# Half of wo's first block on partitions 0 to 63, brought by two transfers of 32 partitions whose source counts in eights

## The chip, the core and the metric

The kernel runs on one core of one Trainium2 chip. The metric is the device time of one execution in microseconds (us). "Engine 0 to 15" means the 16 DMA engines of the core. TensorE is called PE, VectorE DVE, ScalarE ACT, GpSimd POOL and SyncE SP, as in the profile.

## The reference, cut to what matters

One decode step of attention over a long cache, mixed with a gated MLP. The caches are 2 x 268 MB and are read once; all else is small.

```python
def _A_ref(x, k_cache, v_cache, wq, wo):        # B=4, D=1024, H=32, Sk=8192, Dh=128
    q = ...(x @ wq)...
    scores = jnp.einsum("bhqd,bhkd->bhqk", q, k_cache) * (Dh ** -0.5)
    p = _softmax(scores, axis=-1)
    o = jnp.einsum("bhqk,bhkd->bhqd", p, v_cache)
    return o.transpose(...).reshape(B, Sq, H * Dh) @ wo      # wo: 4096 x 1024
...
g = _sigmoid((x * gate_w).sum(-1, keepdims=True))
return g * a + (1 - g) * b
```

## The kernel before

K and V stream through a ring of five slots in SBUF on the SP queue. `wo` comes last, in eight blocks of 512 rows (1 MB each). A block lies on 128 partitions, 4 rows (8 KB) on each; the matching rows of the attention's output are brought to the same partitions by small matmuls with slices of the identity (`o_rows`). Blocks 0 and 1 are queued ahead of the last piece of V, the others behind it, the last two in ever smaller cuts.

```python
    def o_rows(g0, g1):
        n = g1 - g0
        lp = small([P, FR, n, Bn])
        for k in range(WB):                     # WB = 4 heads in a block
            for r in range(FR):                 # FR = 4 rows on a partition
                nc.tensor.matmul(lp[32 * k:32 * k + 32, r], lhsT=identb[:, r:P:FR],
                                 rhs=OT[:, WB * g0 + k:WB * g1:WB, :], start=True, stop=True, skip_group_check=True)
        nc.vector.tensor_copy(out=LT[:, :, g0:g1, :], in_=lp[:])

    def wo_block(g, r0=0, r1=FR):
        home, at = divmod(g, 4)
        if home not in wo_home:
            wo_home[home] = ring[:, slots(1)].rearrange("p (g r n) -> p g r n", g=4, r=FR)
        w = wo_home[home][:, at]
        nc.sync.dma_start(out=w[:, r0:r1].rearrange("p r n -> p (r n)"),
                          in_=wov[:, g, r0:r1].rearrange("p r n -> p (r n)"))
        def use():
            for r in range(r0, r1):
                for n in range(NH):
                    mm_acc(acc[:, n * NB:(n + 1) * NB], LT[:, r, g, :], w[:, r, n * NB:(n + 1) * NB])
        return use
    # ... cut ...
        if (kind, d) == ("v", ND - 1):
            for g in range(2):
                wo_block(g)()
        if kind == "v":
            v_pair(d)
    # ... cut ...
    last = [wo_block(g) for g in range(2, NWB - 2)]
    cuts = [(NWB - 2, 0, 2), (NWB - 2, 2, 4), (NWB - 1, 0, 2), (NWB - 1, 2, 3), (NWB - 1, 3, 4)]
```

Another part matters for one experiment: `keep_weights` drops a weight load of PE that repeats the one before it.

Of the kernel before, what the change touches and what calls it, by code (L numbers as in the profile page):

```python
# [8 lines left out]
BF = mybir.dt.bfloat16  # L9
# [103 lines left out]
def kernel(  # L113
# [15 lines left out]
    nc = tc.nc  # L129
    P = 128  # L130
    Bn, Sq, D = A_x.shape
# [13 lines left out]
    FR = 4  # L145
    FG = F // (P * FR)
    NB = 512
    NH = D // NB
# [8 lines left out]
    const = ctx.enter_context(tc.tile_pool(name="const", bufs=1))  # L157
# [10 lines left out]
    ring = const.tile([P, NS, RING], BF, name="ring")  # L168
# [6 lines left out]
    def turned(rows, n, dtype=BF):  # L175
        t = TB[tb_turn[0] % 3]
        tb_turn[0] += 1
        return t[0:rows, 0:n] if dtype == BF else t[0:rows, 0:2 * n].bitcast(dtype)

    def slots(n):  # L180
        at = turn[0]
        turn[0] = (at + n) % NS
        return at
# [15 lines left out]
    def small(shape, dtype=F32):  # L199
        return mps.tile(shape, dtype, name="small", tag="small")  # L200
# [16 lines left out]
    acc = acc4[0:Bn].rearrange("p z n -> p (z n)")  # L217
# [3 lines left out]
    n = 1  # L221
# [6 lines left out]
    ident = const.tile([P, P], F32)  # L228
# [2 lines left out]
        nc.gpsimd.tensor_copy(out=ident[n:n + 32, n:n + 32], in_=id32[n:n + 32])  # L231
    identb = const.tile([P, P], BF)
    nc.vector.tensor_copy(out=identb[:], in_=ident[:])
    xw_ps = small([P, DT, NX], BF)
    for t in range(DT):
        nc.tensor.transpose(out=xw_ps[:, t, :], in_=x6[:, t:D:DT], identity=identb[0:NX, 0:NX])  # L236
# [4 lines left out]
    for half in range(2):  # L241
        for e in range(2):
            nc.gpsimd.tensor_copy(out=R[:, 2 * half + e].rearrange("p (n j) -> p n j", n=4),
                                  in_=ident[:, 64 * half + e:64 * half + 64:2].unsqueeze(1).to_broadcast([P, 4, 32]))
# [20 lines left out]
    qa = const.tile([P, 4, H, Bn], BF)  # L265
    OT = const.tile([P, H, Bn], BF)
    LT = const.tile([P, FR, H // FR, Bn], BF)
    hT = const.tile([P, FG, FR, Bn], BF)
    sgb = const.tile([P, 2, Bn], F32)
    c12 = const.tile([P, 2, Bn], F32)  # L270

    def mm_acc(out_ap, lhsT, rhs, start=False):
        nc.tensor.matmul(out_ap, lhsT=lhsT, rhs=rhs, start=start, stop=True, skip_group_check=True)  # L273
# [16 lines left out]
    def add_x():  # L290
        xf = turned(Bn, D, F32)
        nc.vector.tensor_copy(out=xf, in_=x6[0:Bn])
        for n in range(NH):
            mm_acc(acc[:, n * NB:(n + 1) * NB], dg[:], xf[:, n * NB:(n + 1) * NB])
# [67 lines left out]
# [4 lines that stand above are left out]
        for k in range(WB):  # L366
            for r in range(FR):
                nc.tensor.matmul(lp[32 * k:32 * k + 32, r], lhsT=identb[:, r:P:FR],  # L368
                                 rhs=OT[:, WB * g0 + k:WB * g1:WB, :], start=True, stop=True, skip_group_check=True)
        nc.vector.tensor_copy(out=LT[:, :, g0:g1, :], in_=lp[:])  # L370

    wo_home = {}

    def wo_block(g, r0=0, r1=FR):

# [12 lines that stand above are left out]
# [35 lines left out]
    def k_pair(d):  # L423
        g, t = divmod(d, GD)
        Z = Zt[d % 2]
        if d == 0:
            spread(0)
        if t == 0:
            S_ps[g] = scp.tile([P, 2, 512], F32, name="S_ps")
        sps = S_ps[g]  # L430
        ks = load_pair(kv_view(A_k_cache, d), RING)
        for n in range(RD):
            kn, c = ks[n // JT], n % JT
            flat_t = turned(P, CJ * P)
            T = flat_t.rearrange("p (j h i e) -> p j h i e", j=CJ, h=2, e=2)
            nc.vector.transpose(out=flat_t.bitcast(U32),  # L436
                                in_=kn[:, c * CJ * Dh:(c + 1) * CJ * Dh].bitcast(U32))
            s = QP - 1 - (RD * t + n)
            for he in range(4):
                half, e = divmod(he, 2)  # L440
                for z in range(2):
                    nc.tensor.matmul(sps[:, z, :], lhsT=Z[:, he, s:s + P], rhs=T[:, 16 * z:16 * z + 16, half, :, e],  # L442
                                     start=(t == 0 and n == 0 and he == 0),
                                     stop=(t == GD - 1 and n == RD - 1 and he == 3))
            if n == JT // 2 and d + 1 < ND:
                spread(d + 1)
            if n == JT:
                flush()
            if n == JT + 2:
                flush_late()  # L450
        if t == GD - 1:
            softmax(g)
# [101 lines left out]
    for kind, d in order:  # L554
        if kind == "k":
            k_pair(d)
            if d in side:
                side[d]()
        if (kind, d) == ("v", ND - 1):
            for g in range(2):  # L560
                wo_block(g)()
        if kind == "v":
            v_pair(d)
        if (kind, d) == ("k", ND // 2):
            add_x()
        if (kind, d) == ("v", ND - 2):
            o_rows(0, GE)
# [5 lines left out]
    flush_late()  # L573
    last.pop(0)()
    o_rows(GE, NWB)
    for use in last:
        use()
# [35 lines left out]
```

## Time and profile before

| | before |
|---|---|
| time, median (range) of 6 runs | 1344.05 us (1343.86 to 1344.24) |
| span of the profiled execution | 1342.2 us |
| PE busy | 77% of the span |
| instruction fetches of 16 KB | 27 |

The page of the kernel before, its slices (one figure for each 1/40 of the span; for DMA the busy share in tenths) and its table of DMA queues (packets, MB, share of 16 engines' time):

```profile
DMA  9999999999999999999999999999999999999997
GB/s 414 436 432 431 439 434 427 445 430 422 445 424 430 442 432 426 438 434 428 438 436 426 432 430 434 436 433 438 428 423 436 430 431 442 436 419 444 419 425 325
...
q1 hardware_dynamic: 14276, 575.69, 99.5%
q8 instruction: 27, 0.44, 0.1%
```

The DMA engines are busy for 90% or more of every slice before the last, so bytes, and how evenly they lie on the engines, set the time. The q8 line: 27 packets, 0.1% of the time.

The end of the chain of waits before (start us, length us, what):

```profile
1321.33 16.11 DMA ring<-in_A_wo_dram
1337.43 0.04 issue
1337.47 1.90 PE acc L273 x8
1339.37 0.02 issue
1339.40 0.57 ACT TB L581
```

The span ends on landings of wo, eight matmuls, a copy, and the output. The landing that is named is that of the third transfer of wo from the end (1337.43 us); the last two land at 1338.1 and 1338.7 us, while the eight matmuls run. All three show the same gaps between the engines. The timeline around block 0 (start us, length us, engine, line, what; in brackets the idle time before it and what ended it):

```profile
1306.32 0.22 DVE L370 CAST LT<-small 128x64 bf16<-128x64 f32 x1 [40.50 <-PE small L368]
1306.60 2.75 PE L273 MATMUL acc<-ring,LT 128*4 128x512 bf16 x12 [0.32 <-DVE LT L370]
...
1308.98 0.39 PE L513 MATMUL o_ps<-ring,PB 128*32 128x512 bf16 x1
...
1313.84 1.24 PE L513 MATMUL o_ps<-ring,PB 128*32 128x512 bf16 x5 [1.23 <-DMA ring<-in_A_v_cache_dram]
```

PE begins on the last V at 1308.98 us and has to wait for data 1.23 us at 1313.84 us.

Two things come from the trace's records and not from a view. A transfer adds 1 to its semaphore for each engine that finishes its share, so the 16 times of these completions show how far apart the engines are. And each packet has a start and a length; on one engine the packets follow each other without a gap. Before, the 16 completions of the last transfer of wo (us):

```
1332.3 1332.3 1332.4 1332.7 1332.9 1332.9 1333.2 | 1335.3 | 1336.9 1337.0 1337.0 1337.0 1337.2 | 1338.5 1338.7 1338.7
```

Seven engines are early, one is 3 us behind the first, and eight are 4.7 to 6.4 us behind. At 38 us the spread was 0.6 us. The lag grows in steps, one for each 16 KB fetch. Such a step, near 302 us (start, end, length in us, bytes, queue):

```
299.691 302.117 2.426 65536 q1      the packet before
302.114 303.173 1.059 16384 q8      the fetch
303.158 306.084 2.926 65536 q1      1.04 us later than without it, and 0.5 us longer
```

So one fetch costs its engine about 1.55 us. Eight engines take the fetches in turn: in the transfers that begin to land at 401, 808 and 1215 us, after 8, 16 and 24 fetches, eight engines are 1.6 to 2.0, 3.2 to 3.5 and 4.7 to 5.0 us behind the first. And 27 = 3 x 8 + 3: at the end five of the eight have three, three have four. PE and its weight loads have 4552 + 2364 = 6916 instructions by the page, or 256 for each of the 27 fetches: these are PE's instructions. The Trainium skill, "Runtime: NRT & Kernel Launch", section "Instruction fetch mechanics", says that instructions come in blocks of 16 KiB, 256 instructions each, and that crossing into the next block is "mostly hidden". The size agrees with this trace.

### The profile page before, as it was taken

The numbers are of one execution on the slowest core, as the hardware profiler recorded it, in microseconds if no ns is written. First come the engines' busy times: TensorE is split into PE (matmuls) and PEld (weight loads), VectorE is DVE, ScalarE is ACT, GpSimd is POOL, SyncE is SP. The second block draws the span as 40 slices with busy tenths as digits, with TensorE's granted clock in tenths as the row PEclk, the third lists the DMA queues.
The fourth block names the chain that finished last, engine by engine and source line by source line (L and its number), as shares of the span: only waits on it lengthen the run. The fifth ranks groups of instructions, "written<-read, shape, count | busy, mean of one in ns | idle before, by whom it ended". The sixth has DMA issues, their size and how long they took to land.

```text
span 1342.2 us, 7696 instructions
## 1 busy us (share of the span) xinstructions
PE 1032.8 (77%) x4552; PEld 227.9 (17%) x2364; DVE 614.4 (46%) x369; ACT 50.6 (4%) x46; POOL 62.8 (5%) x161
## 2 busy tenths in 40 slices
PE   2565878787788687778977779597778679877898
PEld 0111111111111121111211112111111112111221
DVE  2555655545336554335455556046555254556000
ACT  0000100001000010001000010000100010000100
POOL 2000100001000010001000010000100010000100
PEclk9787988888998888889988889888889899888899
DMA  9999999999999999999999999999999999999997
GB/s 414 436 432 431 439 434 427 445 430 422 445 424 430 442 432 426 438 434 428 438 436 426 432 430 434 436 433 438 428 423 436 430 431 442 436 419 444 419 425 325
DMA packets 14316, 576.18 MB, mean 429 GB/s; under 512 B 1598, under 2 KB 1606, under 8 KB 2252
## 3 DMA queue, kind: packets, MB, share of 16 engines
q1 hardware_dynamic: 14276, 575.69, 99.5%
q8 instruction: 27, 0.44, 0.1%
q14 instruction: 5, 0.04, 0.0%
q10 hardware_dynamic: 8, 0.00, 0.0%
HBM read 575.68 MB, written 0.01 MB: 429 GB/s over the span
## 4 chain that ended last, share of the span: by engine, by line
DMA 66%; DVE 21%; PE 11%; another core or an unknown queue 1%; ACT 0%; issue 0%; SPq 0%; DVEq 0%
DMA ring<-in_A_k_cache_dram 58%; DVE TB L436 21%; PE o_ps L513 9%; DMA ring<-in_A_v_cache_dram 5%; DMA x<-in_gate_w_dram 2%; DMA ring<-in_A_wo_dram 1%; PE S_ps L442 1%; ACT PB L484 0%; PE S_ps L307 0%; PE acc L307 0%; PE acc L273 0%; PE small L533 0%; ACT OS L525 0%; PE small L472 0%
## 5 line engine op out<-in xcount | busy, mean ns | idle before, releaser
L436 DVE STREAM_TRANSPOSE TB<-ring 128x2048 uint32<-128x2048 uint32 x256 | 566.9, 2277 | 492.4 <-DMA ring<-in_A_k_cache_dram 491.5
L442 PE MATMUL S_ps<-TB,Z 128*128 128x512 bf16 x2048 | 518.8, 408 | 219.4 <-DVE TB L436 218.9
L513 PE MATMUL o_ps<-ring,PB 128*32 128x512 bf16 x2048 | 461.4, 388 | 52.6 <-DMA ring<-in_A_v_cache_dram 48.1
L442 PEld LDWEIGHTS <-Z 128*128 128x128 bf16 x1024 | 105.4, 103 | 628.0 <-issue 626.4
L513 PEld LDWEIGHTS <-PB 128*32 128x32 bf16 x1024 | 100.7, 98 | 405.1 <-issue 393.7
L421 POOL COPY Z<-qa 32x4 bf16<-32x4 bf16 x128 | 25.6, 200 | 761.6 <-PE S_ps L442 736.0
L486 POOL COPY PB<-PT 32x1024 bf16<-32x1024 bf16 x16 | 30.3, 1892 | 430.3 <-PE o_ps L513 426.2
L467 ACT ACTIVATE PTs<-S_ps,mx 128x1024 bf16<-128x1024 f32 x8 | 8.9, 1114 | 1020.9 <-DVE mx L463 1020.9
L526 DVE SCALAR_TENSOR_TENSOR OS<-o_ps,mE,OS 128x512 f32<-128x512 f32 x8 | 6.0, 751 | 72.2 <-ACT OS L525 72.2
L484 ACT COPY PB<-PT 32x1024 bf16<-32x1024 bf16 x16 | 30.5, 1908 | 1.5 <-DVE PT L469 1.3
L474 DVE RECIPROCAL rinv<-small 128x16 f32<-128x16 f32 x8 | 2.1, 258 | 42.0 <-PE small L472 42.0
L370 DVE CAST LT<-small 128x64 bf16<-128x64 f32 x2 | 0.4, 224 | 42.3 <-PE small L368 42.3
L236 PE MATMUL small<-identb,x 6*128 6x6 bf16 x8 | 0.6, 195 | 22.3 <-DMA x<-in_gate_w_dram 22.3
L457 DVE TENSOR_REDUCE mx<-S_ps 128x1 f32<-128x1024 f32 x8 | 9.8, 1225 | 15.9 <-PE S_ps L442 15.9
L273 PE MATMUL acc<-ring,LT 128*4 128x512 bf16 x64 | 14.8, 379 | 1.7 <-DMA ring<-in_A_wo_dram 1.0
L469 DVE STREAM_TRANSPOSE PT<-PTs 128x1024 bf16<-128x1024 bf16 x8 | 10.0, 1245 | 10.2 <-ACT PTs L467 10.2
L273 PE MATMUL acc<-ring,hT 128*4 128x512 bf16 x56 | 12.2, 379 | 0.0
L525 ACT ACTIVATE OS<-o_ps,mE 128x512 f32<-128x512 f32 x8 | 5.5, 687 | 162.8 <-PE o_ps L513 162.8
L307 PE MATMUL o_ps<-ring,xw 128*4 128x512 bf16 x56 | 5.7, 536 | 5.3 <-DMA ring<-in_B_w_gate_dram 5.3
L533 PEld LDWEIGHTS small<-selg,OS 128*128 128x128 f32 x64 | 9.0, 208 | 4.1 <-issue 3.9
L533 PE MATMUL small<-selg,OS 128*128 128x16 f32 x64 | 8.7, 269 | 0.0
L238 DVE COPY xw<-small 128x48 bf16<-128x48 bf16 x1 | 0.2, 181 | 15.9 <-PE small L236 15.9
(64 smaller groups left out, 67.2 us busy)
## 6 DMA issues: line engine op xcount, KB each, us to landing
ring<-in_A_k_cache_dram SPq DMA_DIRECT2D x14, 4096.0 KB, 34.1
ring<-in_A_v_cache_dram SPq DMA_DIRECT2D x14, 4096.0 KB, 31.4
ring<-in_B_w_gate_dram SPq DMA_DIRECT2D x1, 7168.0 KB, 37.1
ring<-in_B_w_up_dram SPq DMA_DIRECT2D x1, 7168.0 KB, 39.2
ring<-in_B_w_down_dram SPq DMA_DIRECT2D x2, 3584.0 KB, 27.4
ring<-in_A_wo_dram SPq DMA_DIRECT2D x6, 1024.0 KB, 24.7
ring<-in_A_v_cache_dram SPq DMA_DIRECT2D x2, 2048.0 KB, 28.7
ring<-in_A_v_cache_dram SPq DMA_DIRECT2D x4, 1024.0 KB, 24.7
```

Source lines behind the costliest of these rows:

```text
L273: nc.tensor.matmul(out_ap, lhsT=lhsT, rhs=rhs, start=start, stop=True, skip_group_check=True)
L421: nc.gpsimd.tensor_copy(out=Z[at, :, QP - 1 + QP * q], in_=qa[at, :, h0 + q, b])
L436: nc.vector.transpose(out=flat_t.bitcast(U32), in_=kn[:, c * CJ * Dh:(c + 1) * CJ * Dh].bitcast(U32))
L442: nc.tensor.matmul(sps[:, z, :], lhsT=Z[:, he, s:s + P], rhs=T[:, 16 * z:16 * z + 16, half, :, e], start=(t == 0 and n == 0 and he == 0), ...
L457: nc.vector.tensor_reduce(out=mx[:, 0:1], in_=sps[:].rearrange("p z n -> p (z n)"), axis=AX.X, op=ALU.max)
L467: nc.scalar.activation(out=PTs[:], in_=sps[:].rearrange("p z n -> p (z n)"), func=ACT.Exp, bias=negm[:, 0:1], scale=scale, accum_out=rs[:, ...
L469: nc.vector.transpose(out=PT[:].rearrange("p j i -> p (j i)"), in_=PTs[:])
L484: nc.scalar.copy(out=Bv[at, :, :, q, :], in_=Pv[at])
L486: nc.gpsimd.tensor_copy(out=Bv[at, :, :, q, :], in_=Pv[at])
L513: nc.tensor.matmul(o_ps[row:row + NM, e, :], lhsT=PB[:, RD * t + c, z, w].rearrange("p e s j -> p (e s j)"), rhs=vn[:, j0 * Dh:(j0 + 4) * ...
L526: nc.vector.scalar_tensor_tensor(out=o_sb[:], in0=o_ps[:, 1, :], scalar=mE[:, 1:2], in1=o_sb[:], op0=ALU.mult, op1=ALU.add)
L533: nc.tensor.matmul(oT[:, :], lhsT=o_sb[:, q * Dh:(q + 1) * Dh], rhs=selg[:, q].rearrange("p t s -> p (t s)"), start=(q == 0), stop=(q == 3))
```

## The change

The intent, as far as the code shows it: move bytes from engines 8 to 15 to engines 0 to 7. Rows 0 to 255 come by two transfers onto partitions 0 to 63, whose source's outermost dimension has 8 steps; rows 256 to 511 come onto 128 partitions, 2 rows on each. `ident4` orders the rows of the attention's output to match. The diff, cut:

```diff
+    ident4 = const.tile([P, FR, 8, 4], BF)
+    nc.gpsimd.tensor_copy(out=ident4[:], in_=ident[:].rearrange("p (o e r) -> p r e o", o=4, e=8))
...
+        if g0 == 0:
+            lp = small([P, FR + 2, Bn])
+            for k in range(2):
+                for r in range(FR):
+                    nc.tensor.matmul(lp[32 * k:32 * k + 32, r], lhsT=ident4[:, r].rearrange("p e o -> p (e o)"),
+                                     rhs=OT[:, k, :], start=True, stop=True, skip_group_check=True)
+                for r in range(2):
+                    nc.tensor.matmul(lp[64 * k:64 * k + 64, FR + r], lhsT=identb[:, r:P:2], rhs=OT[:, 2 + k, :],
+                                     start=True, stop=True, skip_group_check=True)
+            nc.vector.tensor_copy(out=LT2[0:P // 2, 0:FR], in_=lp[0:P // 2, 0:FR])
+            nc.vector.tensor_copy(out=LT2[:, FR:FR + 2], in_=lp[:, FR:FR + 2])
...
+    def wo_first():
+        wo_home[0] = ring[:, slots(1)].rearrange("p (g r n) -> p g r n", g=4, r=FR)
+        w = wo_home[0][:, 0].rearrange("p r n -> p (r n)")
+        half = P * FR // 2
+        lower = A_wo[0:half].rearrange("(h o e r) n -> h e o (r n)", h=2, e=8, r=FR)
+        for h in range(2):
+            nc.sync.dma_start(out=w[32 * h:32 * h + 32], in_=lower[h])
+        w2 = turned(P, 2 * D)
+        nc.sync.dma_start(out=w2, in_=A_wo[half:2 * half].rearrange("(p r) n -> p (r n)", r=2))
+        def use():
+            ...                              # 8 matmuls on 64 partitions of w, 4 on 128 of w2
+        return use
...
-            for g in range(2):
-                wo_block(g)()
+            wo_first()()
+            wo_block(1)()
```

More of the change, by code (lines that the diff above doesn't have):

```diff
@@ L267 @@
     LT = const.tile([P, FR, H // FR, Bn], BF)
+    LT2 = const.tile([P, FR + 2, Bn], BF)
     hT = const.tile([P, FG, FR, Bn], BF)
@@ L370, in o_rows @@
         nc.vector.tensor_copy(out=LT[:, :, g0:g1, :], in_=lp[:])
-    wo_home = {}
+        if g0 == 0:
[9 more added lines that the diff above has]
+            nc.vector.tensor_copy(out=LT2[:, FR:FR + 2], in_=lp[:, FR:FR + 2])
+    wo_home = {}
+    def wo_first():
[8 more added lines that the diff above has]
+        def use():
+            for r in range(FR):
+                for n in range(NH):
+                    mm_acc(acc[:, n * NB:(n + 1) * NB], LT2[0:P // 2, r, :], w[0:P // 2, r * D + n * NB:r * D + (n + 1) * NB])
+            for r in range(2):
+                for n in range(NH):
+                    mm_acc(acc[:, n * NB:(n + 1) * NB], LT2[:, FR + r, :], w2[:, r * D + n * NB:r * D + (n + 1) * NB])
+        return use
     def wo_block(g, r0=0, r1=FR):
```

## The prediction

> **What bounds the kernel now.** The DMA stream. The page's slices show the DMA engines at 90% or more until the last slice; PE is busy 77%. The chain of waits is 66% DMA, and its end is DMA of wo (16.11 us), eight last matmuls (1.90 us) and the output. The timeline shows PE waiting for landings of V and wo from 1298 us on; after the last V landing PE has about 0.3 us of slack against the last landings of wo.
>
> **The 16 engines do not end together.** The completion records of each transfer (16 increments, one an engine) spread over 0.6 us at 38 us, but over 6.4 us at the end. The last transfer of wo: seven engines at 1332.3 to 1333.2 us, one at 1335.3, five at 1336.9 to 1337.2, three at 1338.5 to 1338.7. The packet records show why: the instruction queue has 27 fetches of 16 KB, spread over eight engines in turn; each costs its engine about 1.55 us (near 302 us: 1.06 us, and the next 64 KB packet takes 2.93 instead of 2.42). Eight engines are therefore three or four fetches behind; one other is 3 us behind through 8 KB fetches. Each engine moves 32 KB in 1.21 us whatever the others do, so the late eight decide.
>
> **What the change does.** Rows 0 to 255 of wo come as two transfers whose source's slowest dimension is 8. The Trainium skill, "DMA: Bandwidth & Descriptors", section "Why a DMA increments its semaphore by 16 and not by 1", says such a transfer runs on the lowest-numbered 8 engines; "The descriptor swizzle" there says engines 0 to 7 are those that serve partitions 0 to 63 anyhow. Rows 256 to 511 lie on 128 partitions with 4 KB each, on all engines. Per engine, block 0 was 64 KB; it becomes 96 KB on engines 0 to 7 and 32 KB on 8 to 15. wo's 8 KB packets take 0.31 us, 4 KB ones 0.16 us: 8 to 15 are relieved by about 1.23 us, 0 to 7 loaded by as much. The profile does not name the late eight. Following packets from the small loads of x at the start, which the rule puts on engines 0 to 3, engine 0 is among the early seven at the end; so I take the late eight to be 8 to 15. Then every late landing after block 0 comes 1.2 us sooner, and the early engines (6 us ahead) absorb theirs.
>
> **What it adds.** PE: 12 small matmuls and 4 more of 0.215 us, with two DVE casts of about 0.2 us, together 1.2 to 1.6 us just before the last V blocks. PE needs 1.75 us for each V megabyte that takes 2.49 us to land, so it catches up before the last V piece. A POOL copy of about 0.3 us at 7 us: free. SP issues two more transfers, some 20 us ahead of need: free.
>
> **Time.** All of the 1.2 us is on the critical path, less up to 0.2 us of PE slack: 1344.08 - 1.1 = 1343.0 us, 8 in 10 between 1342.3 and 1344.3. Faster by over 2%: 0.2%; same: 99.6%; slower: 0.2%.
>
> **What would show it.** Landing spread of the last wo transfer near 4 us instead of 6.4; last landing near 1337.5; PE's matmuls waiting for DMA as before.
>
> **What would make it wrong.** The late eight are 0 to 7 (then 1345.3) or a mix of both halves (then about the same or +1.2); an added fetch on a late engine (+1.5); PE not catching up.

## The result

| | before | changed |
|---|---|---|
| time, median (range) of 6 runs each | 1344.05 us (1343.86 to 1344.24) | 1344.44 us (1343.53 to 1345.30) |
| span of the profiled execution | 1342.2 us | 1343.2 us |

The ratio is 1.0003 (95% interval 0.999 to 1.0016). The median lies 0.14 us outside the predicted range. But the median describes no run: the six times are 1343.53, 1343.76, 1343.82 and 1345.06, 1345.08, 1345.30, two groups 1.5 us apart, all at the same clock (0.894 to 0.902). The kernel before has one group.

The profile after is of a run of the slow group (1345.06). Its queues and the end of its chain:

```profile
q1 hardware_dynamic: 14356, 575.69, 99.4%
q8 instruction: 27, 0.44, 0.1%
```

```profile
1322.27 16.07 DMA ring<-in_A_wo_dram
1338.34 0.04 issue
1338.38 1.90 PE acc L276 x8
1340.28 0.02 issue
1340.30 0.57 ACT TB L616
```

The same chain, 0.9 us later: the landing that ends it is later, and nothing new stands behind it. The timeline around block 0 after:

```profile
1306.77 0.17 DVE L383 CAST LT<-small 64x16 bf16<-64x16 f32 x1
1306.93 0.17 DVE L384 CAST LT<-small 128x8 bf16<-128x8 f32 x1
1306.99 1.89 PE L276 MATMUL acc<-ring,LT 64*4 64x512 bf16 x8
1308.81 1.02 PE L276 MATMUL acc<-TB,LT 128*4 128x512 bf16 x4
...
1310.33 0.39 PE L548 MATMUL o_ps<-ring,PB 128*32 128x512 bf16 x1
...
1314.80 0.38 PE L548 MATMUL o_ps<-ring,PB 128*32 128x512 bf16 x1 [0.85 <-DMA ring<-in_A_v_cache_dram]
```

PE begins on the last V 1.35 us later than before (1310.33 against 1308.98), yet at the next piece it waits for data again, 0.85 us. So the added PE work is absorbed; it does not reach the end.

The completions of the last transfer of wo, before and in the changed kernel's profile. The times are measured; the words beside those of the changed kernel are worked out from the completions of the transfers in eights, shown next, and from the shift of 1.23 us ("relieved" engines have fewer bytes of block 0 than before, "loaded" ones more):

```
before   1332.3 1332.3 1332.4 1332.7 1332.9 1332.9 1333.2 | 1335.3 | 1336.9 1337.0 1337.0 1337.0 1337.2 | 1338.5 1338.7 1338.7
changed  1331.1 1331.7                            two early engines, relieved
         1333.6 1333.7 1334.0 1334.2 1334.3       five early engines, loaded
         1335.5 1335.6 1335.7 1335.8 1336.1       five late engines, relieved
         1336.4                                   the one that was 3 us behind, loaded
         1337.5                                   one late engine, relieved
         1339.6 1339.6                            two late engines, loaded
```

The first transfer in eights has, besides one step of its semaphore at the issue, 8 completions: 1293.92, 1294.03, 1294.33, 1294.54, 1294.59 (five early), 1296.69, and 1298.42 and 1299.95. So it does run on eight engines, and two of these are late ones. The change relieves six late engines and loads two. Relieved and loaded end 2.5 us apart (1331.1 to 1333.6 among the early ones), which is twice the 1.23 us of the prediction. The two loaded late ones end the kernel.

The theory for the experiments: the late eight are two of engines 0 to 7 and six of 8 to 15; the two loaded ones decide; whether one of them has a fourth fetch in an execution makes the two groups. Rivals: the added PE work; a cost of transfers with 32 partitions; some other cause of two groups.

### The profile page after: what moved, and what is told of

Its sections match the earlier page's. It is cut to its first block, busy times and chain, and to the rows that moved or that the text cites. A ratio compares the mean times of both kernels' runs of the same rounds, so it can differ in the third digit from the quotient of the medians.

```text
span 1343.2 us, 7735 instructions
## 1 busy us (share of the span) xinstructions
PE 1036.2 (77%) x4568; PEld 228.1 (17%) x2378; DVE 614.8 (46%) x371; ACT 50.6 (4%) x46; POOL 63.1 (5%) x162
## 4 chain that ended last, share of the span: by engine, by line
DMA 69%; DVE 20%; PE 10%; issue 0%; ACT 0%; SPq 0%; DVEq 0%
DMA ring<-in_A_k_cache_dram 58%; DVE TB L471 20%; PE o_ps L548 7%; DMA ring<-in_A_v_cache_dram 5%; DMA ring<-in_A_wo_dram 3%; DMA ring<-in_B_w_gate_dram 3%; PE S_ps L477 2%; PE o_ps L310 0%; PE acc L310 0%; PE acc L276 0%; PE small L568 0%; PE small L507 0%; DVE OS L561 0%; ACT OS L560 0%; ACT TB L616 0%
## 5 line engine op out<-in xcount | busy, mean ns | idle before, releaser
L276 PE MATMUL acc<-ring,LT 128*4 128x512 bf16 (+1 forms) x64 | 14.9, 378 | 1.5 <-DMA ring<-in_A_wo_dram 0.9
L276 PE MATMUL acc<-ring,hT 128*4 128x512 bf16 x56 | 12.2, 379 | 0.0
```

What stands on the lines that cost most here:

```text
L276: nc.tensor.matmul(out_ap, lhsT=lhsT, rhs=rhs, start=start, stop=True, skip_group_check=True)
```

## The experiments

All ten runs gave the reference's result. The runs of before beside them had medians of 1343.92 (experiments 1 to 4), 1343.97 (5 to 8) and 1343.90 us (9 and 10), 9 runs each.

### 1. The same split, on all sixteen engines (e1_even)

```diff
-        lower = A_wo[0:half].rearrange("(h o e r) n -> h e o (r n)", h=2, e=8, r=FR)
+        lower = A_wo[0:half].rearrange("(h p r) n -> h p (r n)", h=2, r=FR)
...
-                    nc.tensor.matmul(lp[32 * k:32 * k + 32, r], lhsT=ident4[:, r].rearrange("p e o -> p (e o)"),
+                    nc.tensor.matmul(lp[32 * k:32 * k + 32, r], lhsT=identb[:, r:P:FR],
```

> The changed kernel, but the two transfers of 32 partitions count their source in 32 instead of eights, so that they should run on all 16 engines; all of the added matmuls and casts stay. Theory (the late engines are mixed: six of the late eight are relieved by the eights, two are loaded by 1.2 us, and these two decide the end in some runs): no 8-landing transfer in the records, the landing spread at the end is back near 6.4 us, all runs within 0.5 us of each other and within 0.3 us of before (1344.1). Rival (the added PE work ate the gain): 0.5 to 1.3 us over before, as the changed kernel's slow runs, and the spread of runs is small. Rival (transfers of 32 partitions are slow for themselves): as the changed kernel, two groups of runs.

Measured: 1348.53 us (1347.94 to 1348.61), 4.6 us over before. All three expectations failed on the time. The landing spread at the end is back at 6.4 us and all completions come in sixteens, as the theory said; the end itself is later. Busy time in three stretches, of the kernel before and of this one (stretch, its us, busy us of each engine, clock, DMA share, GB/s):

```profile
1290.00:1306.00 16.00, 14.74 (x84) 3.55 (x47) 0.00 (x0) 0.00 (x0) 0.00 (x0) 1.00 0.98 414
1306.00:1326.00 20.00, 17.13 (x89) 3.87 (x48) 0.22 (x1) 0.28 (x1) 0.00 (x0) 1.00 1.01 422
```

```profile
1290.00:1306.00 16.00, 12.43 (x63) 2.86 (x31) 0.00 (x0) 0.00 (x0) 0.00 (x0) 1.00 1.00 309
1306.00:1326.00 20.00, 18.46 (x114) 4.87 (x71) 0.55 (x3) 0.00 (x0) 0.00 (x0) 1.00 1.00 421
```

While these transfers run the engines are as busy as ever (share 1.00 against 0.98) and move 309 GB/s instead of 414; afterwards the rate is the same (421 and 422). The bytes missed are (414 - 309) x 16 us, at 429 GB/s 3.9 us: most of the loss. The packets show how. In the 4 us after 1292 us, 8 KB packets take 0.58 us in the median here and 0.31 in the changed kernel; 32 KB packets of V, in flight at the time, 2.04 instead of 1.22. With 32 partitions over 16 engines each engine writes two partitions; that they are two neighbours is assumed here. The Trainium skill, "SBUF — State Buffer", section "Door 1: The DMA port swizzle", says that partitions 0 to 31 reach 8 of the 16 ports and that four neighbouring partitions share one. By that, two engines write to each port, beside the engine whose own port it is. That lengths nearly double agrees; that it is ports, no record here names. What follows: the eights are not only there to pick engines. They keep each engine on its own partitions (by the mapping that the prediction cites), and the naive form of the same split costs 4.6 us.

### 2. All of block 0 in eights (e2_whole)

Four transfers in eights, onto partitions 0 to 31, 32 to 63, 64 to 95 and 96 to 127; `w2` is gone.

```diff
-        lower = A_wo[0:half].rearrange("(h o e r) n -> h e o (r n)", h=2, e=8, r=FR)
-        for h in range(2):
-            nc.sync.dma_start(out=w[32 * h:32 * h + 32], in_=lower[h])
-        w2 = turned(P, 2 * D)
-        nc.sync.dma_start(out=w2, in_=A_wo[half:2 * half].rearrange("(p r) n -> p (r n)", r=2))
+        rows = A_wo[0:P * FR].rearrange("(h o e r) n -> h e o (r n)", h=4, e=8, r=FR)
+        for h in range(4):
+            nc.sync.dma_start(out=w[32 * h:32 * h + 32], in_=rows[h])
```

> All of block 0 of wo comes by four transfers counted in eights, so that engines 0 to 7 carry 128 KB of it and 8 to 15 none: the shift of load is 64 KB an engine instead of 32. PE has no more matmuls on acc than before. Theory (mixed late engines): the two late engines among 0 to 7 are now 2.5 us later than before; runs in which one of them has four instruction fetches end near 1344.1 + 2.5 = 1346.5, runs in which both have three near 1345.0; the landing spread between the earliest and latest engine near 6.1 + 5.0 = 11 us in a profile of the first kind. If the late eight were all in 8 to 15: 1341.7. If the load of the engines does not matter and PE's added work does: within 0.3 of before.

Measured: 1351.79 us (1350.14 to 1353.18). Inconclusive: it mixes two things. Its third and fourth transfers write partitions 64 to 127 from engines 0 to 7, and in 1295 to 1300 us its 8 KB packets take 0.63 us and V's 32 KB packets 2.46. The first two, on partitions 0 to 63, keep 0.31. The spread near the end, 12.2 us, is close to the 11 us expected (10.0 us in the very last transfer, which was issued after the earliest engine had finished the one before). Experiment 7 does it without the fault.

### 3. The eights onto partitions 64 to 127 (e3_upper)

```diff
-            nc.sync.dma_start(out=w[32 * h:32 * h + 32], in_=lower[h])
+            nc.sync.dma_start(out=w[64 + 32 * h:96 + 32 * h], in_=lower[h])
```

`LT2` and the matmuls move to the same partitions.

> As the changed kernel, but the eights land on partitions 64 to 127. If the engines are chosen by the count (the lowest-numbered eight, whatever the partitions): the eight landings stand as in the changed kernel (five early, one 2.8 us later, two 4.5 to 6 us later), the times in two groups 1343.6 and 1345.2. If the engines belong to the partitions (8 to 15): two early and six late landings, and every run near 1345.3. If crossing ports costs something, the 8 KB packets take longer than 0.31 us and all comes later.

Measured: 1349.21 us (1349.08 to 1350.31). The eight completions of the first transfer are 1295.20, 1295.38, 1295.68, 1295.93, 1296.07, then 1300.97, and 1302.53 and 1303.11: five, one and two, as in the changed kernel. So the count picks the engines, not the partitions. The times expected for that case failed, and the third sentence held: 8 KB packets take 0.62 us, V's 32 KB packets 2.36, and the rate in this stretch is lower still than in experiment 1:

```profile
1290.00:1306.00 16.00, 8.94 (x36) 1.81 (x17) 0.00 (x0) 0.00 (x0) 0.00 (x0) 0.85 0.99 275
```

With experiments 1 and 2 this makes three cases in which engines write partitions that belong to others, all with packets about twice as long, and three (the changed kernel and experiments 7 and 8) in which they don't, with 8 KB packets of 0.31 us.

### 4. Which of engines 0 to 7 are late (e4_probe)

```diff
+            scratch = turned(P, CJ * P)
+            for n in range(1, 8):
+                nc.sync.dma_start(out=scratch[0:n, 256 * n:256 * n + 256], in_=A_wo[0:n, 0:256])
             for g in range(2):
                 wo_block(g)()
```

> The kernel before, with seven small loads of 1, 2, ... 7 rows of 512 bytes in the queue ahead of wo's block 0, which nothing reads. By the rule each runs on as many engines as it has rows, the lowest-numbered. The landings of the one with n rows, less those of the one with n-1, give the lateness of engine n-1, so the two late engines among 0 to 7 get a number. Theory: engine 0 is early (0.4 to 0.5 us after the first), and of 0 to 7 two are 4.5 to 6.5 us behind the first and one about 3 us; time within 2 us of before. If the loads of n rows have other than n late landings, the rule for the number of engines is wrong.

Measured: 1347.72 us, one run of unknown state; 3.8 us over before, more than the 2 us expected. The seven probes held up the SP queue, the engines ran dry (260 GB/s in the stretch from 1290 to 1306 us), and V was issued late. The completions are valid all the same, and each probe has as many late ones as it has rows (us):

```
1 row    1293.12
2 rows   1292.72 1293.30
3 rows   1292.90 1293.31 1293.50
4 rows   1293.07 1293.51 1293.72 1295.98
5 rows   1293.24 1293.39 1293.73 1293.94 1296.16
6 rows   1293.41 1293.60 1293.94 1294.15 1296.34 1299.03
7 rows   1293.61 1293.83 1294.15 1294.36 1296.52 1297.27 1299.22
```

Each row more costs about 0.2 us on the engines before it, and each line has one new time: engine 3 is the one 3 us behind, engine 5 comes at 1299.03, 5.6 us after the first, engine 6 at 1297.27, 3.7 us after the first of its line. Engines 0, 1, 2 and 4 are early, and by the eight completions of the changed kernel so is 7. The two late engines are 5 and 6. This also shows the rule of the Trainium skill ("DMA: Bandwidth & Descriptors", section "Why a DMA increments its semaphore by 16 and not by 1") for 1 to 7 rows: as many engines as rows, always the same first ones. That these are the lowest-numbered is the page's word; the records carry no engine number, so the numbers here are by that rule. The argument needs only that two of the first eight are late.

### 5 and 6. Four fetches for everyone (e5_pad_after, e6_pad_before)

In both kernels the first 1280 repeated weight loads of PE stay in, five blocks of 256 instructions:

```diff
+    extra = 1280
...
                         if free and held == key:
+                            if extra:
+                                extra -= 1
+                                kept.append(i)
                             continue
```

> The changed kernel with 1280 weight loads more (redundant ones that it otherwise drops, kept from the start of the program on), so that PE fetches 32 blocks of instructions instead of 27: every one of the eight fetching engines then has four. Theory (the two groups of times come from whether engines 5 and 6, which are loaded by the change and fetch instructions, have three or four fetches in an execution): no fast group any more, all runs between 1344.9 and 1345.7 and within 0.5 us of each other, the landings of the late engines within 0.6 us among those relieved and among those loaded, the two loaded ones 2.5 us behind the six relieved. Rival (two groups from something else, such as the state of HBM or the clock): the two groups, 1343.7 and 1345.2, remain.

> The same 1280 weight loads more in the kernel before. Theory: in the kernel before some engine has four fetches in every execution, so four on all of them change nothing: within 0.4 us of before (1343.9), spread of runs as before; this is also the control for the cost of the added loads. Rival (the added loads or their fetches cost time by themselves): over 0.5 us slower.

Measured, changed kernel padded: 1345.23 us, all five between 1345.06 and 1345.48. Kernel before padded: 1344.04 us (1343.85 to 1344.13), against 1343.97. Both times are as the theory said. The queue table of the padded changed kernel, and of the padded kernel before:

```profile
q8 instruction: 32, 0.52, 0.2%
```

```profile
q8 instruction: 32, 0.52, 0.2%
```

With 32 = 4 x 8 fetches no engine is spared, and the fast group is gone. The added loads themselves cost nothing that shows (the control, 0.07 us). In the padded changed kernel the last transfer lands at 1337.1 to 1337.8 us on the late engines that are relieved and at 1339.6 and 1339.7 on the two loaded: 1.8 to 2.5 us behind (2.5 was expected). In the padded kernel before, all eight late engines land it at 1338.4 to 1338.6 us, where they were split into five and three. So the two groups of the changed kernel follow the fetch count of engines 5 and 6.

### 7. Twice the shift, all on partitions 0 to 63 (e7_dose)

```diff
+        w2 = turned(P // 2, FR * D)
+        rows = A_wo[0:P * FR].rearrange("(h o e r) n -> h e o (r n)", h=4, e=8, r=FR)
+        for h in range(4):
+            nc.sync.dma_start(out=(w, w2)[h // 2][32 * (h % 2):32 * (h % 2) + 32], in_=rows[h])
```

> All of block 0 by four transfers counted in eights, all on partitions 0 to 63 this time, so no engine writes to partitions of another: engines 0 to 7 carry 128 KB of block 0, 8 to 15 none. Theory: 8 KB packets stay at 0.31 us; engines 5 and 6 are 2.5 us later than before, the six late ones of 8 to 15 2.5 us earlier; runs with four fetches on 5 or 6 near 1346.4, runs with three on both near 1344.7; two groups 1.5 to 1.7 us apart, both 1.0 to 1.3 us above the two groups of the changed kernel. If the late eight decided as predicted blind (8 to 15): 1341.5. If the contention in the second experiment came from eights as such and not from partitions 64 to 127: near 1351 again.

Measured: 1344.99, 1345.04, 1346.34, 1346.55 and 1347.47 us, median 1346.34. Packets of 8 KB stay at 0.31 us. Two runs stand 0.3 us above the lower value expected (1344.7), two at the upper (1346.4). The fifth, 1347.47, fits neither and has no profile. Double the shift, and the distance above before doubles in the slow group (2.5 us against 1.2); the fast group turns from 0.3 us below before into 1.0 above, because two loaded engines with three fetches now end behind any relieved one with four (in the profile of the run at 1344.99, 1339.2 and 1339.5 us against 1336.1). Against the prediction's picture, in which more shift would be better, this is the plainest evidence.

### 8. A quarter of the block, on engines 0 to 3 (e8_quarter)

Engines 5 and 6 are out of the reach of a transfer that counts in fours. Rows 0 to 127 come in fours onto partitions 0 to 15 and 32 to 47; the rest needs no reordering, since the rows of a head already lie on 128 partitions:

```diff
+        rows = A_wo[0:P].rearrange("(h o e r) n -> h e o (r n)", h=2, e=4, r=FR)
+        for h in range(2):
+            nc.sync.dma_start(out=w[32 * h:32 * h + 16], in_=rows[h])
+        w2 = turned(P, 3 * D)
+        nc.sync.dma_start(out=w2.rearrange("p (j n) -> p j n", j=3), in_=A_wo[P:4 * P].rearrange("(j p) n -> p j n", p=P))
...
+                    mm_acc(acc[:, n * NB:(n + 1) * NB], OT[:, 1 + r, :], w2[:, r * D + n * NB:r * D + (n + 1) * NB])
```

> Only the first 128 rows of wo come by a transfer on few engines, and it counts in fours: engines 0 to 3 (three early ones and the one 3 us behind) carry 64 KB of them on their own partitions 0 to 15 and 32 to 47; the other 384 rows of block 0 lie on all 128 partitions in 2 KB pieces. Engines 0 to 3 are loaded by 1.8 us, all the others, the late eight with them, relieved by 0.5 to 0.6 us. Theory: one group of runs, 0.4 to 0.6 us below before (1343.3 to 1343.6), last landing on a late engine still. Rival (the split by itself, more transfers and matmuls, costs time): at or above before.

Measured: 1343.67 us (1343.57 to 1344.01) against 1343.97. One group, 0.3 us below before; 0.4 to 0.6 were expected. Ratio 0.9998, interval 0.9986 to 1.0011.

### 9 and 10. The changed kernel and the quarter once more (e9_changed_again, e10_quarter_again)

> The changed kernel once more, unchanged, beside the next one on one chip: only to count its runs. Theory: again two groups, near 1343.7 and near 1345.2, with nothing between 1344.1 and 1344.9; with eight fetching engines in turn, three of them with a fourth fetch and two neighbours loaded, about half of the runs in each. Rival (two groups were a chance of six runs): a single spread around 1344.4.

> The version with 128 rows on engines 0 to 3 once more, because its first five runs (median 1343.67 against 1343.97) left 0.3 us, less than the 0.4 to 0.6 expected. Theory: one group, median 0.2 to 0.6 us below before on this chip, and no run in the changed kernel's slow group. Rival: the 0.3 us were noise, median within 0.1 us of before.

Measured, changed kernel: 1343.60, 1343.69, 1343.77, 1344.14 and 1345.21 us. One run is in the slow group, three in the fast one, and one at 1344.14 lies between them, where none was expected. Over both sessions: four slow, six fast, one between. Its profile this time fell on a fast run (1343.60), so the same kernel can be read in both groups. The end of its chain:

```profile
1320.82 16.09 DMA ring<-in_A_wo_dram
1336.92 0.04 issue
1336.96 1.90 PE acc L276 x8
1338.86 0.02 issue
1338.88 0.57 ACT TB L616
```

The whole tail is 1.4 us earlier than in the profile of the slow run (1338.88 against 1340.30). The late engines' completions of the last transfer in the two:

```
fast run   relieved: 1335.7 to 1336.6 (three; engine 3, loaded, is among them), 1337.3 1337.4 1337.5    loaded (5 and 6): 1338.1 1338.2
slow run   relieved: 1335.5 to 1336.1 (five; engine 3, loaded, at 1336.4), 1337.5                       loaded (5 and 6): 1339.6 1339.6
```

In the fast run the three engines with a fourth fetch are all relieved ones; in the slow run two of the three are engines 5 and 6. That is the difference of 1.4 us between runs of one kernel.

Measured, quarter: 1343.58 us (1343.50 to 1343.81) against 1343.90: 0.3 us below again, and one group. All ten runs of it lie between 1343.50 and 1344.01, with the 18 runs of before beside them between 1343.73 and 1344.06. It is the only version that is below before in every session and has no slow group, by 0.02%; the interval of one session (0.9985 to 1.0012) doesn't settle so little.

## Why the prediction was wrong

- **What bounds the kernel: right.** DMA to the end, with PE waiting for landings before and after.
- **The lag of eight engines through instruction fetches, 1.55 us each: right.** Padding to 32 fetches did what the theory said.
- **The two transfers run on engines 0 to 7, 1.23 us more there and 1.23 less on 8 to 15: right.** Eight completions, and relieved and loaded 2.5 us apart.
- **The added PE work is absorbed: right.** 1.35 us later at the last V, and waiting for data 4.5 us after that.
- **The step that failed:** "engine 0 is among the early seven at the end; so I take the late eight to be 8 to 15". One engine was identified and seven were inferred. The runs showed engines 5 and 6 late, with six of 8 to 15. The prediction named this case among those that would make it wrong ("a mix of both halves (then about the same or +1.2)"), and that is what came, one after the other from run to run. The signs that it named show the same: instead of a landing spread near 4 us and a last landing near 1337.5 us, the profile of the slow run has 8.5 us and 1339.6, that of the fast run 7.0 us and 1338.2.
- **What stands in its place, as a sum:** before, a late engine with four fetches lands at 1338.5 to 1338.7 us. Changed, with a fourth fetch on engine 5 or 6: 1338.7 + 1.23 = 1339.9 expected, 1339.6 measured, and 1.1 us on the time of the profiled runs (1345.06 against 1343.99). Changed, with three on both: a late engine with three lands at 1336.9 to 1337.2 before, + 1.23 = 1338.1 to 1338.4 expected, 1338.1 and 1338.2 measured. This is 0.5 us earlier than before, and 0.3 to 0.4 us on the time.
- **A sentence that holds only in part:** "Each engine moves 32 KB in 1.21 us whatever the others do". In the changed kernel it held (1.22 us); in experiments 1 to 3, where engines wrote other engines' partitions, 32 KB took 2.04 to 2.46 us.
- **What stays open:** why the turn of the fetches begins at another engine from run to run; the runs at 1344.14 (experiment 9) and 1347.47 (experiment 7), which fit no group; and whether the doubled packets come from SBUF ports, which only the page says.

## What to carry to other kernels

Where the DMA engines are busy to the end, look at the completions of one transfer engine by engine, and move bytes only once every engine that gets more is known to be early: a shift that relieves six late engines and loads two ends on the two. Let a transfer of few partitions run on the engines that serve these partitions anyhow: in experiments 1 to 3, where it did not, its packets and those of its neighbours took about twice as long. And when a median falls between two groups of runs, first find what differs between runs of the same kernel.

## What the Trainium skill lacked or had wrong

- "Runtime: NRT & Kernel Launch", section "Instruction fetch mechanics": it calls the cost of a block boundary mostly hidden and doesn't say that the block takes time on a DMA engine that carries data. Here each 16 KB block costs one engine 1.55 us (1.06 for the fetch, 0.5 for a longer packet after it), PE's 27 blocks go to eight engines in turn, and the engines stand 6.4 us apart at the end.
- No page says which of the sixteen engines bring PE's instructions. Here engines 5, 6 and six of 8 to 15 do. Engine 3 is about 3 us behind too; its lag grows by 0.9 us three times, each after an 8 KB fetch of another queue (at 108, 564 and 991 us), which is the likely cause (not tried).
- "DMA: Bandwidth & Descriptors", section "Latency and other measured facts": it calls engines 7 and 15 usually slower, and limits its guess at the cause to transfers issued from GpSimd. It lacks transfers issued from SP, as here: engine 7 is early and engines 5 and 6 late (5.6 and 3.7 us behind the first in experiment 4).
- The same page, section "Why a DMA increments its semaphore by 16 and not by 1": it names the lowest-numbered engines as seen for 16, 10, 2 and 1. The runs show as many late completions as rows for 1 to 7, and eight for a count of eight.
- "SBUF — State Buffer", section "Door 1: The DMA port swizzle", gives the rate of a transfer by itself. It has no figure for what such a transfer does to others in flight: 32 partitions over 16 engines took 8 KB packets from 0.31 to 0.58 us and V's 32 KB packets from 1.22 to 2.04 us, and the core from 414 to 309 GB/s.
